# Light convolution and gated MLP on one core: first w_in columns loaded plainly, first-tile transposes ahead, tap products dealt out, early casts on GpSimd

## The chip, the cores and the metric

The kernel runs on one core of a Trainium2 chip. The metric is the device time of one execution in microseconds, lower is better. A core has TensorE (PE, with its weight loads shown as PEld), VectorE (DVE), ScalarE (ACT), GpSimd (POOL) and SyncE (SP); SP, ACT and POOL issue DMAs.

## The reference

```python
# _attn_ref: x [8, 4096, 192], weight [8 heads, 7 taps]
w = weight - np.max(weight, axis=-1, keepdims=True)
w = np.exp(w)
w = w / (np.sum(w, axis=-1, keepdims=True) + 1e-09)
x_pad = np.concatenate([np.zeros((B, pad, D)), x], axis=1)      # pad = 6
x_unf = x_pad[:, idx, :].reshape(B, S, K, H, group)
out = np.einsum('hk,bskhg->bshg', w, x_unf)
# _moe_ref: w_in [192, 2048], w_out [2048, 192], beta [2048]
h = x @ w_in
g = h * (1.0 / (1.0 + np.exp(-beta * h)))
return (g @ w_out).astype(np.float32)
```

A causal convolution of seven taps along the sequence, with a softmax over the taps of each head, is followed by two matrix products over 32768 tokens with a gated activation between them.

## The kernel before

The tokens are cut into two halves (streams s = 0 and 1) of 16384, and these into tiles of 512. Each tile is worked in steps: step 0 has 128 tokens of each stream, step 1 another 128, step 2 has 256 (these three make tile 0), then come steps of 256 up to token 2048 and steps of 512 after it. The 192 channels are split as 64 x 3 (`NK = 3`), so that 64 partitions hold one stream.

A step consists of mm1 (x @ w_in into PSUM tiles `ph`), the activation on ACT (`g`), and mm2 (g @ w_out into PSUM tiles `po`), which runs one step behind mm1 and is dealt out between its groups. There are two `ph` and two `po` buffers. When a pair of 128-token blocks has had all its mm2 products, DVE copies `po` into `o_sb` and SP stores it.

**Tile 0 is made on PE.** x0 holds its four blocks of 128 tokens of both streams. `transpose_0` turns a block with three PE transposes, `take_0` copies it into `xr[b]`, `halo_0` copies its last six columns ahead of the next block, and `conv_0` multiplies with seven tap diagonals (`diag[k]`, made by DVE from `etap`, the exponentials of the taps), accumulating in PSUM. `evac_0` scales the result by the inverse sum of the taps into `xcp`. Steps 0 to 2 use `mm1_pair`: PE's upper and lower 64 rows work on two different column groups of w_in at a time, u and u + 8, so only half s of w_in_s need hold column half s.

**Later tiles are made on DVE.** `load_x(j)` loads tile j as fp32 (`xf`, two buffers), `cast_x(j)` casts and reorders it into `xb` (two buffers), four DMA transposes (`transpose_x`, on SP) put it into `xt`, and `conv_ops` makes the convolution in seven passes: the first is a product (L291), the others multiply and add (`scalar_tensor_tensor`, L293, with inputs xt and acc). The last writes `xc`, which mm1 reads.

**Order.** Nearly every instruction is pinned in program order, so the order is written by hand. For the steps after 2, DVE's convolutions are in the list `work`. `vector_work` takes items from it by a budget of nanoseconds per PE group and an estimated cost of each item; o_sb copies are put into DVE's queue where PE's program reaches the end of a pair. Tile 1's cast and transposes are written out in step 1, those of tile 2 and later are the items of `fetch`.

**Head.** POOL's queue loads w_in in four casting DMAs (fp32 to bf16), then w_out as fp32 (`w_out_f`), then tile 1; later it issues four copies of w_in_s from one half of the partitions to the other (`copy_w_in`), which only mm1 of step 3 and later needs. DVE scales w_out_f by 1/beta into `w_out_s`, slice by slice (`scale_w_out`); all 16 slices are read by the first half of mm2 of step 0. beta comes to its place by a PE transpose. `warm` issues products of zeros while PE has nothing to do.

Of the kernel before, what the change touches and what calls it, by code (L numbers as in the profile page):

```python
# [19 lines left out]
def kernel(  # L20
# [24 lines left out]
    def pin(ins):  # L45

        return tc.keep_in_program_order(ins)
# [33 lines left out]
    def cast_x(j, s, b0=0, b1=NB, eng=None):  # L81
        if j not in xbf_of:
            xbf_of[j] = xbf_pool.tile([128, NB, NK, NS, Q], BF16, name="xb")
        pin((eng or nc.vector).tensor_copy(  # L84
            xbf_of[j][:, b0:b1, :, s, :].rearrange("p b k q -> p k b q"),
            xf_of[j][:, b0:b1, s, :].rearrange("p b (q k) -> p k b q", k=NK)))
# [29 lines left out]
    taps = consts.tile([H, K], FP32, name="taps")  # L116
    pin(nc.sync.dma_start(out=taps, in_=weight))
    x0 = consts.tile([128, NB, NS, D], FP32, name="x0")
    pin(nc.scalar.dma_start(out=x0[:, 0, 1, :], in_=xs[1, 0:128, :]))
    pin(nc.sync.dma_start(out=x0[:, 0, 0, :], in_=xs[0, 0:128, :]))  # L120
    beta16 = consts.tile([NF, 128], FP32, name="beta16")
    pin(nc.sync.dma_start(out=beta16, in_=moe_beta.rearrange("(c p) -> c p", p=128)))

# [4 lines left out]
    scrap = consts.tile([128, 1], FP32, name="scrap")  # L128
    pin(nc.scalar.activation(scrap, one, AF.Exp))

    HF = F // 2
    load_w_in(0, 0, 512)

    def load_x0(b, eng=nc.gpsimd):
        pin(eng.dma_start(out=x0[:, b, :, :],
                          in_=xs[:, 128 * b:128 * b + 128, :].rearrange("s p d -> p s d")))

    for b in range(1, NB):
        load_x0(b, nc.sync)


    sel = consts.tile([H, NS, H, Q // H], FP32, name="sel")
    pin(nc.gpsimd.memset(sel, 0.0))
    pin(nc.gpsimd.affine_select(out=sel, in_=sel, compare_op=ALU.not_equal, fill=1.0, base=0,
                                pattern=[[0, NS], [-1, H], [0, Q // H]], channel_multiplier=1))
    ident = consts.tile([128, 128], FP32, name="ident")
    pin(nc.gpsimd.memset(ident, 0.0))
    pin(nc.gpsimd.affine_select(out=ident, in_=ident, compare_op=ALU.not_equal, fill=1.0,
                                base=0, pattern=[[-1, 128]], channel_multiplier=1))
    for f in range(0, HF, 512):  # L150
        for s in range(NS):
            if f or s:
                load_w_in(s, HF * s + f, HF * s + f + 512)
    for c in range(0, NF, 4):
        pin(nc.gpsimd.dma_start(out=w_out_f[:, c:c + 4, :], in_=w_out_v[:, c:c + 4, :]))
    for b in (0, 2):
        for s in range(NS):
            load_x(1, s, b, b + 2, nc.gpsimd)
    for f in range(0, HF, 512):
        for s in range(NS):  # L160
            copy_w_in(s, HF * s + f, HF * s + f + 512)
    for s in range(NS):
        cast_x(1, s, 2, 4, nc.gpsimd)


    xr = [consts.tile([128, NK, PAD + 128], FP32R, name=f"xr{b}") for b in range(NB)]
# [4 lines left out]
    def po_tile():  # L171
        return psum_o.tile([128, 2, TILE], FP32, name="po")
# [29 lines left out]
    def transpose_0(bank, b):  # L202
        t = bank[:, 0:NK * 128].rearrange("p (k t) -> p k t", k=NK)
        v = x0[:, b, :, :].rearrange("p s d -> p (s d)").rearrange("p (m k) -> p k m", k=NK)
        for kk in range(NK):
            pin(nc.tensor.transpose(t[:, kk, :], v[:, kk, :], ident))  # L206
        return t

    def take_0(t, b, act=False):

        if act:
            pin(nc.scalar.activation(xr[b][:, :, PAD:], t, AF.Copy))
        else:
            pin(nc.vector.tensor_copy(xr[b][:, :, PAD:], t))  # L214

    def halo_0(t, b):
        dst = xr[b + 1][:, :, 0:PAD] if b + 1 < NB else xt_of[0][:, :, TILE + LEAD - PAD:]
        pin(nc.vector.tensor_copy(dst, t[:, :, 128 - PAD:]))

    def conv_0(cv, b):  # L220

        for k in range(K):
            for s in range(NS):
                pin(nc.tensor.matmul(  # L224
                    cv[s][:, 0:NK * 128], diag[half_of(s), k, :, :].rearrange("p s q -> p (s q)"),
                    xr[b][half_of(s), :, k:k + 128], start=(k == 0), stop=(k == K - 1)))
# [10 lines left out]
    def banks(po):  # L237
        return [po[:, 0, :], po[:, 1, :]]

    new_xt(0)  # L240
    po01 = po_tile()
    t0_ = transpose_0(po01[:, 0, :], 0)
    take_0(t0_, 0, act=True)
    po_b = po_tile()
    beta_ps = po_b[:, 1, 0:NF]
    pin(nc.tensor.transpose(beta_ps, beta16, ident[0:NF, 0:NF]))
    beta = consts.tile([128, NF], FP32, name="beta")
    pin(nc.vector.tensor_copy(beta, beta_ps))
    for k in range(2, K):
        make_diag(k)  # L250
    rsum = consts.tile([128, 1], FP32, name="rsum")
    pin(nc.vector.reciprocal(rsum, tsum))
    warm(3, 128)
    pin(nc.scalar.activation(scrap, one, AF.Silu))
    b0 = [cv0[:, 0, :], po_b[:, 0, :]]
    conv_0(b0, 0)
    evac_0(b0, 0, 0, nc.scalar)
    evac_0(b0, 0, 1, nc.vector)
    warm(5, 128)
# [4 lines left out]
    halo_0(t0_, 0)  # L264

    def scale_w_out(c):
        pin(nc.vector.tensor_scalar_mul(w_out_s[:, c, :], w_out_f[:, c, :], rbeta[:, c:c + 1]))  # L267
# [122 lines left out]
    def fetched(j):  # L390
        for b in range(NB):
            transpose_x(j, b)
        if (j + 2) * TILE < TS:
            for s in range(NS):
                load_x(j + 2, s)

    def fetch(i, j):
        return [(i, 850, lambda s=s: cast_x(j, s)) for s in range(NS)] + [(i, 0, lambda: fetched(j))]

    work = []  # L400
    for i in range(NP, n_steps):
# [18 lines left out]
    for i in range(n_steps):  # L420
        plan = mm2_plan(i - 1) if i else [[] for _ in range(NF)]
        g_of[i] = g_pool.tile([128, NF, NS, TILE], BF16, name="g")
        if i == 0:
            for u in range(NF // 2):
                mm1_pair(0, u)
                if u == 0:
                    t = transpose_0(po01[:, 1, :], 1)
                    take_0(t, 1)
                    halo_0(t, 1)
                elif u == 1:  # L430
                    cv = banks(po_tile())
                    conv_0(cv, 1)
                    for s in range(NS):
                        evac_0(cv, 1, s, nc.vector)
                elif u == 2:
                    po23 = po_tile()
                    t = transpose_0(po23[:, 0, :], 2)
                    take_0(t, 2)
                    halo_0(t, 2)
                elif u == 4:  # L440
                    cv = banks(po_tile())
                    conv_0(cv, 2)
                    for s in range(NS):
                        evac_0(cv, 2, s, nc.vector)
                elif u == 6:
                    t = transpose_0(po23[:, 1, :], 3)
                    take_0(t, 3)
                    halo_0(t, 3)
                if u >= 4:
                    for c in range(2 * (u - 4), 2 * (u - 3)):  # L450
                        scale_w_out(c)
            continue
        if i < NP:
            for u in range(NF // 2):
                mm1_pair(i, u)
                if i == 1 and u == 0:
                    for c in range(8, 12):
                        scale_w_out(c)
                    cv = banks(po_tile())
                    conv_0(cv, 3)  # L460
                    for c in range(12, NF):
                        scale_w_out(c)
                    for s in range(NS):
                        evac_0(cv, 3, s, nc.vector)
                for t in plan[2 * u] + plan[2 * u + 1]:
                    mm2(i - 1, *t)
                if i == 1 and u == 4:
                    for s in range(NS):
                        cast_x(1, s, 0, 2)
                    for b in range(2):  # L470
                        transpose_x(1, b)
                if i == 2:
                    vector_work(i, 1300, flush=u == NF // 2 - 1)
            if i == 1:
                for s in range(NS):
                    load_x(2, s)
                for b in range(2, NB):
                    transpose_x(1, b)
# [40 lines left out]
```

## Time and profile before

| | |
|---|---|
| time, median of three | 697.3 us (696.92 to 697.62) |
| the profiled execution's own time | 697.36 us |
| its span, first to last instruction | 695.6 us |
| PE busy | 686.9 us (99%) |
| DVE busy | 541.8 us (78%) |
| ACT busy | 587.2 us (84%) |
| POOL busy | 13.7 us (2%) |
| first mm1 product | at 9.0 us, its second half at 9.7 us |
| first product of step 3 | at 36.0 us |

The page gives each engine's busy time over the whole span. A busy PE is not a PE at its peak, since products are pipelined and their ends are modelled. A share over the whole span hides that the first 60 us have other limits than the rest, so the first 60 us are read by themselves: in the chain of waits (what released what, followed back from the end), in the busy time of stretches, and in the timeline of single instructions.

### The profile page before, as it was taken

How to read it: one execution, taken by the hardware profiler on the slowest of the kernel's cores; microseconds unless marked ns; L12 is line 12 of the kernel's file. 1: busy time of each engine (PE TensorE's matmuls, PEld its weight loads, DVE VectorE, ACT ScalarE, POOL GpSimd, SP SyncE). 2: the span in 40 equal slices, each digit the busy share in tenths (PEclk: the TensorE clock that was granted, in tenths of full speed). 3: DMA queues.
4: the chain of work that ended last, by engine and by line, in shares of the span. 5: the costliest groups of instructions: out<-in, count | busy, mean ns of one | idle time of the engine just before them, and what ended most of it. 6: DMA issues, size and time to landing. Idle time of an engine off the chain costs nothing.

```text
span 695.6 us, 25420 instructions
## 1 busy us (share of the span) xinstructions
PE 686.9 (99%) x11559; PEld 538.6 (77%) x11559; DVE 541.8 (78%) x901; ACT 587.2 (84%) x600; POOL 13.7 (2%) x26
## 2 busy tenths in 40 slices
PE   8999999999999999999999999999999999999998
PEld 6699996777777777777777777777777777777777
DVE  4799999999988788778798778797788797785002
ACT  5899999888888888888888888888888888888881
POOL 7000000000000000000000000000000000000000
PEclk9999999999999999999999999999999999999999
DMA  9654433443423334233334233334323342211112
GB/s 228 142 132 115 116 102 100 106 125 104 131 70 104 99 104 115 75 89 98 98 105 115 72 90 100 98 104 116 78 79 104 98 105 70 60 36 47 36 37 69
DMA packets 121196, 67.33 MB, mean 97 GB/s; under 512 B 55024, under 2 KB 120384, under 8 KB 121088
## 3 DMA queue, kind: packets, MB, share of 16 engines
q1 hardware_dynamic: 119152, 61.67, 32.8%
q0 software_dynamic: 1792, 3.93, 2.4%
q8 instruction: 90, 1.47, 0.9%
q14 instruction: 18, 0.15, 0.1%
q10 hardware_dynamic: 144, 0.10, 0.1%
HBM read 28.32 MB, written 25.17 MB: 77 GB/s over the span
## 4 chain that ended last, share of the span: by engine, by line
PE 92%; DVE 5%; DMA 1%; issue 1%; SPq 0%; POOL 0%; DVEq 0%; POOLq 0%
PE po L360 45%; PE ph L323 45%; DVE acc L293 3%; PE po L383 2%; DMA w_in_s<-in_moe_w_in_dram 1%; DVE w_out_s L267 1%; DVE xb L84 1%; PE po L224 0%; DVE acc L291 0%; DMA xt<-xb 0%; SPq L95 0%; DVE o_sb L368 0%; PE ph L310 0%; DVE xcp L235 0%; PE po L206 0%
## 5 line engine op out<-in xcount | busy, mean ns | idle before, releaser
L326 ACT ACTIVATE g<-ph,beta 128x1024 bf16<-128x1024 f32 (+1 forms) x544 | 560.8, 1039 | 85.0 <-PE ph L323 81.2
L360 PEld LDWEIGHTS <-g 64*128 64x128 bf16 x7936 | 361.1, 94 | 94.6 <-issue 1.3
L360 PE MATMUL po<-w_out_s,g 64*128 64x192 bf16 x7936 | 427.1, 243 | 0.7 <-DVE o_sb L368 0.5
L323 PE MATMUL ph<-xc,w_in_s 64*128 64x512 bf16 (+1 forms) x3264 | 419.0, 357 | 0.7 <-DVE xc L293 0.7
L293 DVE SCALAR_TENSOR_TENSOR acc<-xt,tapn,acc 128x512 f32<-128x512 bf16 (+1 forms) x450 | 315.4, 764 | 0.9
L323 PEld LDWEIGHTS <-w_in_s 64*128 64x128 bf16 x3264 | 167.7, 94 | 47.5 <-PE po L360 0.9
L368 DVE COPY o_sb<-po 128x384 f32<-128x384 f32 x124 | 69.1, 557 | 129.0 <-PE po L360 127.1
L293 DVE SCALAR_TENSOR_TENSOR xc<-xt,tapn,acc 128x512 bf16<-128x512 bf16 (+1 forms) x90 | 64.2, 765 | 0.2
L84 DVE CAST xb<-xf 128x768 bf16<-128x768 f32 (+1 forms) x62 | 49.0, 831 | 0.0
L291 DVE TENSOR_SCALAR acc<-xt,tapn 128x512 f32<-128x512 bf16 (+1 forms) x90 | 40.5, 501 | 3.0 <-DMA xt<-xb 1.9
L314 ACT ACTIVATE g<-ph,beta 128x256 bf16<-128x256 f32 (+1 forms) x48 | 22.0, 562 | 5.6 <-PE ph L310 5.2
L310 PE MATMUL ph<-xcp,w_in_s 64*128 64x256 bf16 (+1 forms) x144 | 14.5, 306 | 2.1 <-ACT g L314 1.5
L310 PEld LDWEIGHTS <-w_in_s 64*128 64x128 bf16 x144 | 6.9, 94 | 5.9 <-issue 3.4
L383 PE MATMUL po<-w_out_s,g 128*128 128x192 bf16 x128 | 10.7, 246 | 0.0
L383 PEld LDWEIGHTS <-g 128*128 128x128 bf16 x128 | 10.5, 98 | 0.2 <-issue 0.2
L386 DVE COPY o_sb<-po 128x192 f32<-128x192 f32 x8 | 2.9, 358 | 7.6 <-PE po L383 7.6
L235 DVE TENSOR_SCALAR xcp<-po,rsum 128x384 bf16<-128x384 f32 x7 | 4.0, 611 | 4.5 <-PE po L224 4.5
L224 PE MATMUL po<-xr,diag 64*128 64x384 f32 x49 | 7.1, 379 | 0.3 <-DVE xr L214 0.2
L224 PEld LDWEIGHTS po<-xr,diag 64*128 64x128 f32 x49 | 5.7, 204 | 1.1 <-DVE xr L214 1.1
L282 DVE COPY xt<-xt 128x18 bf16<-128x18 bf16 x28 | 4.7, 166 | 0.0
L267 DVE TENSOR_SCALAR w_out_s<-w_out_f,rbeta 128x192 bf16<-128x192 f32 x16 | 4.5, 353 | 0.0
L178 PE MATMUL ph<-zeros 128*128 128x256 bf16 (+1 forms) x16 | 3.1, 363 | 1.1 <-DVE xr L167 1.1
(44 smaller groups left out, 36.9 us busy)
## 6 DMA issues: line engine op xcount, KB each, us to landing
out_dram<-o_sb SPq DMA_DIRECT2D x124, 192.0 KB, 2.7
xf<-in_x_dram SPq DMA_DIRECT2D x60, 384.0 KB, 4.3
xt<-xb SPq DMA_TRANSPOSE x124, 2.4
w_out_f<-in_moe_w_out_dram POOLq DMA_DIRECT2D x4, 384.0 KB, 8.4
w_in_s<-in_moe_w_in_dram POOLq DMA_DIRECT2D x4, 192.0 KB, 6.6
xf<-in_x_dram POOLq DMA_DIRECT2D x4, 192.0 KB, 7.7
w_in_s<-w_in_s POOLq DMA_DIRECT2D x4, 192.0 KB, 7.0
out_dram<-o_sb SPq DMA_DIRECT2D x8, 96.0 KB, 1.6
```

Source lines behind the costliest of these rows:

```text
L84: pin((eng or nc.vector).tensor_copy(xbf_of[j][:, b0:b1, :, s, :].rearrange("p b k q -> p k b q"), xf_of[j][:, b0:b1, s, :].rearrange("p b ...
L224: pin(nc.tensor.matmul(cv[s][:, 0:NK * 128], diag[half_of(s), k, :, :].rearrange("p s q -> p (s q)"), xr[b][half_of(s), :, k:k + 128], sta ...
L267: pin(nc.vector.tensor_scalar_mul(w_out_s[:, c, :], w_out_f[:, c, :], rbeta[:, c:c + 1]))
L291: pin(nc.vector.tensor_scalar_mul(a, src, w))
L293: pin(nc.vector.scalar_tensor_tensor(out=xc_of[i][:, k0:k1, 0:n] if k == K - 1 else a, in0=src, scalar=w, in1=a, op0=ALU.mult, op1=ALU.add))
L310: pin(nc.tensor.matmul(ph[:, h, 0:NS * n], w_in_s[half_of(h), kk, ts(fcs[h], 128)], xc_of[i][half_of(h), :, kk, :], start=(kk == 0), stop= ...
L314: pin(nc.scalar.activation(g_of[i][:, fcs[h], :, 0:n], ph[:, h, 0:NS * n].rearrange("p (s t) -> p s t", s=NS), AF.Silu, scale=beta[:, fcs[ ...
L323: pin(nc.tensor.matmul(ph[:, s, 0:n], w_in_s[half_of(s), kk, ts(fc, 128)], xc_of[i][half_of(s), kk, 0:n], start=(kk == 0), stop=(kk == NK ...
L326: pin(nc.scalar.activation(g_of[i][:, fc, :, 0:n], ph[:, :, 0:n], AF.Silu, scale=beta[:, fc:fc + 1]))
L360: pin(nc.tensor.matmul(po[:, q, 0:D], g_of[i][r, fc, s, ts(b, 128)], w_out_s[r, fc, :], start=(phase == 0 and fc == 0), stop=(phase == 1 a ...
L368: pin(nc.vector.tensor_copy(o_sb, po[:, :, 0:D]))
L383: pin(nc.tensor.matmul(po[:, 0, 0:D], g_of[i][:, fc, s, ts(b, 128)], w_out_s[:, fc, :], start=(fc == 0), stop=(fc == NF - 1)))
```

## The change

- The first 256 columns of each half of w_in are loaded as fp32 by SP's queue into `w_in_f` and cast into w_in_s by DVE. POOL's casting loads shrink to 384 columns each, and POOL makes `ident` and `sel` ahead of them.
- x0's block 0 comes by one DMA of ACT's queue for both streams, blocks 1 to 3 by two DMAs of SP's queue behind w_in_f; beta16 comes last there.
- beta's transpose goes behind conv_0 of block 0, into the idle `ph` tile. The transposes of blocks 1, 2 and 3 run ahead of the first pair, behind pair 0 and behind pair 1 of step 0. Two `po` tiles, pa and pb, serve all of tile 0's transposes and convolutions.
- conv_0 of blocks 1 and 2 is cut by taps into pieces behind the pairs of step 0 (1, 3, 3 and 2, 3, 2 taps), that of block 3 into 4 and 3 behind pairs 3 and 4 of step 1. The scalings of w_out are placed anew.
- The casts of tile 1 are all on POOL: the first two ahead of the w_in copies, the other two behind them. Tile 1's transposes and tile 2's load move to the end of step 0.
- The casts of tiles 2, 3 and 4 go from DVE to POOL, and the planner counts them as 0 ns in place of 850 each.

```diff
-    pin(nc.scalar.dma_start(out=x0[:, 0, 1, :], in_=xs[1, 0:128, :]))
-    pin(nc.sync.dma_start(out=x0[:, 0, 0, :], in_=xs[0, 0:128, :]))
+    pin(nc.scalar.dma_start(out=x0[:, 0, :, :], in_=xs[:, 0:128, :].rearrange("s p d -> p s d")))
+    HF = F // 2
+    FP = 256
+    w_in_f = consts.tile([128, NK, FP], FP32, name="w_in_f")
+    for s in range(NS):
+        pin(nc.sync.dma_start(out=w_in_f[half_of(s), :, :], in_=w_in_v[:, :, HF * s:HF * s + FP]))
+    for s in range(NS):
+        pin(nc.sync.dma_start(out=x0[:, 1:, s, :],
+                              in_=xs[s, 128:TILE, :].rearrange("(b p) d -> p b d", p=128)))
...
-    for f in range(0, HF, 512):
+    for f0, f1 in ((FP, FP + 384), (FP + 384, HF)):
         for s in range(NS):
-            if f or s:
-                load_w_in(s, HF * s + f, HF * s + f + 512)
+            load_w_in(s, HF * s + f0, HF * s + f1)
...
-    def conv_0(cv, b):
-
-        for k in range(K):
+    def conv_0(cv, b, k0=0, k1=K):
+
+        for k in range(k0, k1):
...
+    pa = po_tile()
+    t = transpose_0(pa[:, 0, :], 0)
+    take_0(t, 0, act=True)
+    warm(4, 128)
     for k in range(2, K):
         make_diag(k)
     rsum = consts.tile([128, 1], FP32, name="rsum")
     pin(nc.vector.reciprocal(rsum, tsum))
-    warm(3, 128)
+    halo_0(t, 0)
+    for s in range(NS):
+        pin(nc.vector.tensor_copy(w_in_s[half_of(s), :, HF * s:HF * s + FP], w_in_f[half_of(s), :, :]))
+    for s in range(NS):
+        cast_x(1, s, 0, 2, nc.gpsimd)
+    for f in range(0, HF, 512):
+        for s in range(NS):
+            copy_w_in(s, HF * s + f, HF * s + f + 512)
+    for s in range(NS):
+        cast_x(1, s, 2, 4, nc.gpsimd)
...
+    beta_ps = idle[:, 1, 0:NF]
+    pin(nc.tensor.transpose(beta_ps, beta16, ident[0:NF, 0:NF]))
+    beta = consts.tile([128, NF], FP32, name="beta")
+    pin(nc.vector.tensor_copy(beta, beta_ps))
+    t = transpose_0(pa[:, 0, :], 1)
+    take_0(t, 1)
+    halo_0(t, 1)
...
     def fetch(i, j):
-        return [(i, 850, lambda s=s: cast_x(j, s)) for s in range(NS)] + [(i, 0, lambda: fetched(j))]
+        eng = nc.gpsimd if j <= 4 else nc.vector
+        return [(i, 850 if eng is nc.vector else 0, lambda s=s: cast_x(j, s, eng=eng)) for s in range(NS)] + [(i, 0, lambda: fetched(j))]
...
+            cv1, cv2, cv3 = banks(pb), banks(pa), banks(pb)
             for u in range(NF // 2):
                 mm1_pair(0, u)
                 if u == 0:
-                    t = transpose_0(po01[:, 1, :], 1)
-                    take_0(t, 1)
-                    halo_0(t, 1)
-                elif u == 1:
-                    cv = banks(po_tile())
-                    conv_0(cv, 1)
-                    for s in range(NS):
-                        evac_0(cv, 1, s, nc.vector)
-                elif u == 2:
-                    po23 = po_tile()
-                    t = transpose_0(po23[:, 0, :], 2)
+                    t = transpose_0(pb[:, 0, :], 2)
                     take_0(t, 2)
                     halo_0(t, 2)
...
+                elif u == 1:
+                    t = transpose_0(pa[:, 0, :], 3)
                     take_0(t, 3)
                     halo_0(t, 3)
+                    conv_0(cv1, 1, 0, 1)
+                elif u == 2:
+                    conv_0(cv1, 1, 1, 4)
+                elif u == 3:
+                    conv_0(cv1, 1, 4, K)
+                    for s in range(NS):
+                        evac_0(cv1, 1, s, nc.vector)
...
+            for b in range(2):
+                transpose_x(1, b)
+            for s in range(NS):
+                load_x(2, s)
+            for b in range(2, NB):
+                transpose_x(1, b)
             continue
```

The piece of steps 4 to 7 of the loop over u, and step 1's loop, follow the same manner as listed above.

More of the change, by code (lines that the diff above doesn't have):

```diff
@@ L129 @@
     pin(nc.scalar.activation(scrap, one, AF.Exp))
[L131 to L139, printed above, removed]
+    ident = consts.tile([128, 128], FP32, name="ident")
+    pin(nc.gpsimd.memset(ident, 0.0))
+    pin(nc.gpsimd.affine_select(out=ident, in_=ident, compare_op=ALU.not_equal, fill=1.0,
+                                base=0, pattern=[[-1, 128]], channel_multiplier=1))
     sel = consts.tile([H, NS, H, Q // H], FP32, name="sel")
@@ L145 @@
                                 pattern=[[0, NS], [-1, H], [0, Q // H]], channel_multiplier=1))
[L146 to L149, printed above, removed]
-    for f in range(0, HF, 512):
+    for f0, f1 in ((FP, FP + 384), (FP + 384, HF)):
         for s in range(NS):
-            if f or s:
-                load_w_in(s, HF * s + f, HF * s + f + 512)
+            load_w_in(s, HF * s + f0, HF * s + f1)
     for c in range(0, NF, 4):
@@ L158 @@
             load_x(1, s, b, b + 2, nc.gpsimd)
-    for f in range(0, HF, 512):
-        for s in range(NS):
-            copy_w_in(s, HF * s + f, HF * s + f + 512)
-    for s in range(NS):
-        cast_x(1, s, 2, 4, nc.gpsimd)
     xr = [consts.tile([128, NK, PAD + 128], FP32R, name=f"xr{b}") for b in range(NB)]
@@ L240 @@
     new_xt(0)
[L241 to L248, printed above, removed]
+    pa = po_tile()
+    t = transpose_0(pa[:, 0, :], 0)
+    take_0(t, 0, act=True)
+    warm(4, 128)
     for k in range(2, K):
@@ L252 @@
     pin(nc.vector.reciprocal(rsum, tsum))
-    warm(3, 128)
+    halo_0(t, 0)
[8 more added lines that the diff above has]
+        cast_x(1, s, 2, 4, nc.gpsimd)
     pin(nc.scalar.activation(scrap, one, AF.Silu))
-    b0 = [cv0[:, 0, :], po_b[:, 0, :]]
+    pb = po_tile()
+    b0 = [cv0[:, 0, :], pb[:, 0, :]]
     conv_0(b0, 0)
@@ L258 @@
     evac_0(b0, 0, 1, nc.vector)
-    warm(5, 128)
+    beta_ps = idle[:, 1, 0:NF]
[5 more added lines that the diff above has]
+    halo_0(t, 1)
     rbeta = consts.tile([128, NF], FP32, name="rbeta")
@@ L263 @@
     pin(nc.vector.tensor_scalar_mul(tapn, etap, rsum))
-    halo_0(t0_, 0)
     def scale_w_out(c):
@@ L426 @@
                 if u == 0:
-                    t = transpose_0(po01[:, 1, :], 1)
-                    take_0(t, 1)
-                    halo_0(t, 1)
-                elif u == 1:
-                    cv = banks(po_tile())
-                    conv_0(cv, 1)
-                    for s in range(NS):
-                        evac_0(cv, 1, s, nc.vector)
-                elif u == 2:
-                    po23 = po_tile()
-                    t = transpose_0(po23[:, 0, :], 2)
+                    t = transpose_0(pb[:, 0, :], 2)
                     take_0(t, 2)
                     halo_0(t, 2)
[L440 to L446, printed above, removed]
+                elif u == 1:
+                    t = transpose_0(pa[:, 0, :], 3)
                     take_0(t, 3)
                     halo_0(t, 3)
-                if u >= 4:
-                    for c in range(2 * (u - 4), 2 * (u - 3)):
-                        scale_w_out(c)
+                    conv_0(cv1, 1, 0, 1)
[5 more added lines that the diff above has]
+                        evac_0(cv1, 1, s, nc.vector)
+                elif u == 4:
+                    conv_0(cv2, 2, 0, 2)
+                elif u == 5:
+                    conv_0(cv2, 2, 2, 5)
+                    for c in range(4):
+                        scale_w_out(c)
+                elif u == 6:
+                    conv_0(cv2, 2, 5, K)
+                    for s in range(NS):
+                        evac_0(cv2, 2, s, nc.vector)
+                elif u == 7:
+                    for c in range(4, 8):
+                        scale_w_out(c)
+            for b in range(2):
+                transpose_x(1, b)
+            for s in range(NS):
+                load_x(2, s)
+            for b in range(2, NB):
+                transpose_x(1, b)
             continue
@@ L455 @@
                 mm1_pair(i, u)
-                if i == 1 and u == 0:
-                    for c in range(8, 12):
+                if i == 1 and u < 2:
+                    for c in range(8 + 4 * u, 12 + 4 * u):
                         scale_w_out(c)
[L459 to L462, printed above, removed]
+                elif i == 1 and u == 3:
+                    conv_0(cv3, 3, 0, 4)
+                elif i == 1 and u == 4:
+                    conv_0(cv3, 3, 4, K)
                     for s in range(NS):
-                        evac_0(cv, 3, s, nc.vector)
+                        evac_0(cv3, 3, s, nc.vector)
                 for t in plan[2 * u] + plan[2 * u + 1]:
                     mm2(i - 1, *t)
[L467 to L471, printed above, removed]
                 if i == 2:
@@ L474 @@
             if i == 1:
[L475 to L478, printed above, removed]
                 for s in range(NS):
```

## The prediction

> **What bounds the kernel now.** I read the chain of waits first, from 23 to 60 us, then the busy time by stretch, then single instructions in the timeline.
>
> ```profile
> PE 92%; DVE 5%; DMA 1%; issue 1%; SPq 0%; POOL 0%; DVEq 0%; POOLq 0%
> ```
>
> The 5% is not spread out. The chain lies on VectorE almost without a break from 16 us to 58 us, and on PE from there to the end:
>
> ```profile
> 23.24 0.81 DVE xb L84 x2
> 24.07 2.23 SPq L95
> 26.35 2.36 DMA xt<-xb
> 28.79 0.76 DVE acc L291
> ...
> 35.78 1.60 DVE xb L84 x2
> ...
> 44.62 1.60 DVE xb L84 x2
> ```
>
> Columns are start, length, what. Tile 1 is cast on DVE at 23.2, transposed by DMA, and from 28.8 the tap convolutions run; the casts of tiles 2 and 3 stand between them, on the chain. By stretch (length, then PE, PEld, DVE, ACT, POOL busy):
>
> ```profile
> 36.00:47.60 11.60, 11.06 (x232) 10.87 (x233) 11.39 (x16) 11.29 (x18) 0.00 (x0) 1.00 0.43 108
> 58.50:75.00 16.50, 16.50 (x354) 16.48 (x355) 16.15 (x20) 16.25 (x25) 0.00 (x0) 1.00 0.44 122
> ```
>
> DVE is full at first, PE afterwards: after 58.7 us PE has no gap worth counting. What this change is worth is therefore how much earlier or later PE enters its closed stretch. It is held up last here (the bracket gives idle time before and its releaser):
>
> ```profile
> 36.01 0.50 PE L323 MATMUL ph<-xc,w_in_s 64*128 64x256 bf16 x6 [0.71 <-DVE xc L293]
> 47.59 0.51 PE L360 MATMUL po<-w_out_s,g 64*128 64x192 bf16 x8 [0.53 <-DVE o_sb L368]
> ```
>
> At 47.59 the second product of step 3 needs the PSUM tile that o_sb number 3 empties; that copy stands in DVE's queue behind the convolutions. A last gap of 0.3 us follows at 58.4.
>
> **What the Trainium skill says.** "SBUF — State Buffer", § Who interferes with whom: VectorE and GpSimd share one pair of SBUF ports under an exclusive lock. A DVE instruction in a two-port mode, or one with two SBUF inputs against a GpSimd instruction that reads SBUF, waits for the whole of the other. The trace agrees for the first kind. A w_out_s scaling takes 0.309 us (median); this one met a POOL cast:
>
> ```profile
> 19.72 0.75 POOL L84 CAST xb<-xf 128x384 bf16<-128x384 f32 x1 [0.63 <-DMA xf<-in_x_dram]
> 19.83 0.76 DVE L267 TENSOR_SCALAR w_out_s<-w_out_f,rbeta 128x192 bf16<-128x192 f32 x1
> ```
>
> It ended 0.11 us after the cast. POOL got in although DVE's scalings stand back to back. The second kind, the taps (L293 reads xt and acc, both in SBUF), never meets a POOL instruction in this trace. "GPSIMD Engine Reference", § 7 prices a read with a step over 8 bytes at 2.9 cycles per element of a 1.2 GHz clock: 1.86 us for the 768 elements of a cast here (step 12 bytes), an estimate. The trace has 0.687 and 0.748 us for 384 elements, so I take 1.3 us for 768, with 1.2 to 1.5 as ends. "VectorE: DVE Perf Modes", § The perf-mode tier table, gives fp32 SBUF copies up to 2x; the cast of 768 strided elements measured 0.845 us on DVE. I take 0.45 to 0.85 us for one of the two new w_in casts.
>
> **The change, part by part.** The sum is against the profiled execution: span 695.6, time 697.36 us, 0.06 above the median of 697.3.
>
> *Head (0 to 9.7 us).* Before, PE waited 0.59 us for beta, conv_0 of block 0 began at 5.54, and the first pair could not finish its second half before the w_in load landed at 9.64. After: beta's transpose goes behind conv_0, which then starts at about 4.9 (xr from ACT ends 4.83) and ends at about 7.5 (2.6 us as before). The diagonals follow at 0.24 us each from 4.09, ahead of PE. On DVE the halo and two w_in casts (0.9 to 1.7 us) come before the evacuation, so xcp is ready at 7.9 to 8.4. First pair: 8.7, a gain of about 1.0. Unknown is when x0's blocks 1 to 3 and beta land: SP's queue now has two w_in loads ahead of them; the last such load landed 6.0 us after its issue at 3.1, now two issue at about 2.0 and 2.5, so 7.5 to 9.2. Ends of the gain: 0 and 1.3. One warm run of five and one of three give way to one of four; that saves nothing of weight, as PE works then anyway. POOL makes ident first, but tap_ps still needs sel, at about 2.6 as now. The same w_in bytes are read ahead of w_out_f, by two queues in place of one, so w_out_f lands where it did, about 12.7 to 16.4. At nothing I cost x0's block 0 as one ACT DMA (two halves landed by 3.2 before; the transposes wait for the tap product at 3.4 anyway) and the shared PSUM tiles pa and pb (0.3 us of waits for DVE's takes is in step 0 below; without the cover of ACT's activations it would be up to 1 us).
>
> *Step 0.* Eight pairs at 0.33, two transposes at 0.45, two convs at 1.37 dealt out by taps: 6.3 us of PE, 6.6 with bank waits, against 18.12 - 9.68 = 8.4. ACT no longer idles 1.25 us behind a whole conv. Step 1 starts at 15.3.
>
> *Step 1.* Now the w_out chain binds: evacuation of block 2 ends at 15.9, twelve scalings at 0.23 make 18.7. But tile 1's first casts are now POOL's, and land-bound at 17.0 to 18.4: two locks of 0.7 put the last slice at 20.1, and mm2 of step 0 waits for it (it ended at 22.5 before). Left on PE: five pairs 1.65, conv 1.37, second half of mm2 1.4: 24.5 against 26.06, a gain of 1.55.
>
> *Convolution of tile 1.* Before, it waited for the last evacuation, two casts and two DMA transposes until 28.79. Now POOL casts by 18.4, transposes issue then and take the 4.7 us of before (24.07 to 28.79), up to 6.7 while the DMA engines are still full: 23.1 to 25.1. o_sb number 1 ends at 25.0. So DVE starts the taps at 25.2, **3.6 us earlier**. POOL's w_in copies slide to 18.4-20.9, needed only at step 3: free. o_sb 1's store now stands behind tile 2's loads and two transposes on SP, at about 27 as before; four o_sb buffers cover it. Step 2 is ACT's 16 activations, 9.35 us, so step 3 can't start before 33.75 (35.3 before).
>
> *DVE up to o_sb number 3.* The compiled order puts it behind conv 3 (7.0), first product and two taps (2.85), o_sb 2 (0.46), four taps (4.2), halo (0.15), product and four taps (4.95), itself (0.5): 20.1 us, so 45.3 against PE's 47.59. The fetch now costs the planner nothing, so four more taps stand ahead of this copy than before; that is why 3.6 became 2.3.
>
> *The six casts of tiles 2, 3, 4 on POOL.* They leave 3.2 us of casts (tiles 2, 3) off DVE ahead of that copy, already counted in the 20.1. When do they run? Loads of tile 2 issue at about 22.1 behind the first transposes and land 3.5 and 5.0 us later, as before: 25.7 and 27.6. Tile 3's follow o_sb 1's store: 30 and 32. Tile 4's come behind tile 2's four transposes (5.9 us on SP): 39.5 and 41. All six fall into the taps ahead of o_sb 3. If a tap waits for a POOL cast, each costs DVE 1.3, six 7.8, less about 0.6 where one falls on a first product or a PSUM copy, which have one SBUF input or none: 7.2. Then conv 3 ends at about 37, step 3 starts there and not at 33.75, and o_sb 3 ends at 52.5: PE is **4.9 later** than at 47.59, 4.6 with the gap at 58.4 gone. After it DVE has no POOL beside it and keeps up (conv 6 and o_sb 5 end at about 63.0, needed at 63.4), so the loss stays constant. Sum: 697.36 + 4.6 = **702.0**.
>
> **Rivals.** (A) *Taps are locked out by POOL's casts*: the case above. For it: the collision shown and the page's plain rule. Against: no tap has met one here. 699.8 to 704.0, from locks of 1.1 to 1.5 us and one us either way in the start of the taps.
> (B) *Taps run beside POOL.* If the rule doesn't hold for this operation, or DVE keeps the lock through its row of taps, the casts are hidden: o_sb 3 at 45.3, -2.3, and -0.3 for the later gap: **694.7** (693.5 to 695.8). It decides between A and B at 2.6/6 = 0.43 us of lock per cast. For it: POOL is empty from 20 us on and the taps start 3.6 us earlier.
> (C) *A part is locked*, as where casts land beside evacuations or come after o_sb 3: two of six, 2.6 us, 697.4, no change.
> (D) *The head gives nothing back*, because x0 lands after 9.2 behind the w_in loads: moves A or B up by up to 1 us, less where the w_out chain binds.
>
> **How the numbers follow.** A 0.66, B 0.24, C 0.10; D lies in their widths. 0.2% is 1.4 us, about what a measurement of this kernel can tell from no change. Faster takes B without its upper end, 0.23; same 0.09; slower the rest, 0.68. The range must reach B to leave out no more than 2 in 10: 694.2 to 704.0; A's own is 699.8 to 704.0. Predicted: 702.0.
>
> **What would show it.** Right: taps (L294) of 2.0 to 2.4 us beside POOL casts, in place of 1.02; PE waiting for xc at about 37 and for o_sb at about 52; the first tap near 25. Wrong: taps of 1.02 us beside the casts, or the wait for o_sb at 45. The head is wrong if the first pair starts after 9.6, the w_out chain if mm2 of step 0 runs before 19.

## The result and the profile after

The changed kernel is slower. Its median is 706.26 us (703.83 to 706.52, four runs) against 697.46 us for the kernel before (696.92 to 698.49, four runs): ratio 1.0117, 95% interval 1.0091 to 1.0142. The profiled execution took 706.52 us at a span of 704.7, so it is 9.1 us of span above the one of before; it is the slowest of the four. The forecast had the sign and the lock of VectorE by GpSimd, missed how late the first loads land, and had half of the amount.

From the page of the kernel after: the shares of the chain, then three groups (busy us, mean ns | idle before, releaser).

```profile
PE 94%; DVE 3%; DMA 1%; issue 1%; SPq 0%
L361 PE MATMUL po<-w_out_s,g 64*128 64x192 bf16 x7936 | 429.2, 243 | 3.1 <-DVE o_sb L369 2.9
L84 POOL CAST xb<-xf 128x768 bf16<-128x768 f32 (+1 forms) x10 | 11.9, 1217 | 19.4 <-DMA xf<-in_x_dram 19.3
L256 PE MATMUL ph<-ident,beta 16*128 16x16 f32 x1 | 0.3, 282 | 5.1 <-DMA beta<-in_moe_beta_dram 5.1
```

DVE's share of the chain fell from 5% to 3%, which alone would look like progress. Two waits have grown: one tiny transpose of beta idles PE for 5.1 us (0.59 before), and one o_sb copy holds the second product of step 3 up for 2.9 us (0.53 before). The chain of waits of the kernel after, start, length, what:

```profile
3.73 8.79 DMA beta<-in_moe_beta_dram
...
20.55 0.61 DVE xcp L225
21.16 1.98 DVE w_out_s L268 x4
...
32.22 0.76 DVE acc L292
...
37.22 1.88 DVE acc L294
39.16 1.75 issue
40.91 0.75 DVE acc L292
```

Its first long piece is an 8 KB load, and it enters the taps at 32.22, where the chain of before entered them at 28.79. The same places in PE's timeline of the kernel after (the bracket gives idle time before and its releaser):

```profile
12.56 0.28 PE L256 MATMUL ph<-ident,beta 16*128 16x16 f32 x1 [5.07 <-DMA beta<-in_moe_beta_dram]
...
13.62 0.82 PE L311 MATMUL ph<-xcp,w_in_s 64*128 64x256 bf16 x6
...
41.13 0.50 PE L324 MATMUL ph<-xc,w_in_s 64*128 64x256 bf16 x6 [0.54 <-DVE xc L294]
...
55.39 0.51 PE L361 MATMUL po<-w_out_s,g 64*128 64x192 bf16 x8 [2.88 <-DVE o_sb L369]
```

The first pair starts at 13.62 (8.98 and 9.68 before), step 3 at 41.13 (36.01 before), and the wait for o_sb number 3 ends at 55.39 (47.59 before). Six products take 0.82 us at 13.62 and 0.50 at 41.13.

**The taps beside POOL.** A tap is one multiply-and-add pass of `conv_ops`. VectorE's timeline and then GpSimd's, of the kernel after:

```profile
33.01 6.08 DVE L294 SCALAR_TENSOR_TENSOR acc<-xt,tapn,acc 128x768 f32<-128x768 bf16 x5
39.12 1.86 DVE L294 SCALAR_TENSOR_TENSOR xc<-xt,tapn,acc 128x768 bf16<-128x768 bf16 x1
...
44.14 4.59 DVE L294 SCALAR_TENSOR_TENSOR acc<-xt,tapn,acc 128x768 f32<-128x768 bf16 x3
```

```profile
28.90 2.47 POOL L84 CAST xb<-xf 128x768 bf16<-128x768 f32 x2 [6.34 <-DMA xf<-in_x_dram]
36.53 3.65 POOL L84 CAST xb<-xf 128x768 bf16<-128x768 f32 x2 [5.16 <-DMA xf<-in_x_dram]
43.73 3.13 POOL L84 CAST xb<-xf 128x768 bf16<-128x768 f32 x2 [3.56 <-DMA xf<-in_x_dram]
```

Tile 2's casts ran alone, 1.22 us each, ahead of the taps. Each of the other four met a tap: four taps took 1.87, 1.86, 1.64 and 1.87 us in place of 1.02, together 3.2 us more (taken singly; the lines above have them in groups). The casts grew as well (3.65 and 3.13 for two). A lock means here what these lines show: a VectorE instruction that meets a GpSimd cast takes longer, and mostly the cast does too.

Last, the busy time by stretch (length, then PE, PEld, DVE, ACT, POOL, granted clock, DMA share, GB/s):

```profile
32.20:55.30 23.10, 18.93 (x335) 15.63 (x331) 22.52 (x23) 20.55 (x33) 6.78 (x4) 1.00 0.59 155
56.50:59.90 3.40, 3.40 (x42) 3.20 (x38) 3.33 (x5) 1.98 (x4) 0.00 (x0) 0.50 0.33 101
60.00:75.00 15.00, 15.00 (x324) 14.98 (x321) 12.48 (x15) 14.85 (x23) 0.00 (x0) 1.00 0.21 53
```

DVE is nearly full from 32.2 to 55.3 (22.52 of 23.10 us), as it was before; PE is full from 60 on. Between them lies what before did not have: 3.4 us with PE's granted clock at half (0.50), soon behind the o_sb wait.

**The 9.1 us in one sum.** Taps start at 32.22 against 28.79: +3.4. From there to the end of o_sb number 3 it takes 23.1 us (55.34 - 32.22) against 18.7 (47.53 - 28.79): +4.4, of which the locks are 3.2 and the rest, 1.2 to 1.3, is four more taps ahead of the copy (about 4.2) less the four casts of tiles 2 and 3 that left DVE (about 3.0). So PE leaves its wait 7.8 later. The gap of 0.3 us at 58.4 is gone, and half a clock for 3.4 us costs the remaining 1.6.

### The profile page after: what moved, and what is told of

The parts are those of the page before. It is cut to its first block, busy times and chain, and to the rows that moved or that the text cites. A ratio compares the mean times of both kernels' runs of the same rounds, so it can differ in the third digit from the quotient of the medians.

```text
span 704.7 us, 25423 instructions
## 1 busy us (share of the span) xinstructions
PE 690.3 (98%) x11555; PEld 540.6 (77%) x11555; DVE 542.5 (77%) x895; ACT 587.6 (83%) x600; POOL 24.1 (3%) x34
## 4 chain that ended last, share of the span: by engine, by line
PE 94%; DVE 3%; DMA 1%; issue 1%; SPq 0%
PE po L361 46%; PE ph L324 45%; DVE acc L294 2%; PE po L384 2%; DMA beta<-in_moe_beta_dram 1%; PE ph L311 1%; PE po L214 0%; PE po L197 0%; DVE acc L292 0%; DVE w_out_s L268 0%; DVE xcp L225 0%; SPq L124 0%; SPq L126 0%; DVE o_sb L369 0%; SPq L117 0%
## 5 line engine op out<-in xcount | busy, mean ns | idle before, releaser
L84 DVE CAST xb<-xf 128x768 bf16<-128x768 f32 x54 | 43.3, 844 | 0.0
L84 POOL CAST xb<-xf 128x768 bf16<-128x768 f32 (+1 forms) x10 | 11.9, 1217 | 19.4 <-DMA xf<-in_x_dram 19.3
L214 PE MATMUL po<-xr,diag 64*128 64x384 f32 x49 | 9.1, 428 | 0.0
```

Of the source, the lines that this page charges most:

```text
L84: pin((eng or nc.vector).tensor_copy(xbf_of[j][:, b0:b1, :, s, :].rearrange("p b k q -> p k b q"), xf_of[j][:, b0:b1, s, :].rearrange("p b ...
L214: pin(nc.tensor.matmul(cv[s][:, 0:NK * 128], diag[half_of(s), k, :, :].rearrange("p s q -> p (s q)"), xr[b][half_of(s), :, k:k + 128], sta ...
```

## The experiments

Twelve further kernels were run. Each ratio is against runs of the kernel before on the same chip (medians there 697.46 to 698.24); the places in us come from one profiled execution each.

| kernel | median us | ratio, 95% interval | taps start | step 3 starts | o_sb 3 ends |
|---|---|---|---|---|---|
| before (profiled once) | 697.46 | 1 | 28.79 | 36.01 | 47.53 |
| after | 706.26 | 1.0117, 1.0091 to 1.0142 | 32.22 | 41.13 | 55.34 |
| e1_casts_dve | 700.93 | 1.0042, 1.0030 to 1.0054 | 32.01 | 40.30 | 50.77 |
| b1_casts_pool | 705.32 | 1.0103, 1.0082 to 1.0124 | 29.53 | 38.42 | 54.55 |
| e2_pairs_first | 704.45 | 1.0103, 1.0077 to 1.0128 | 32.92 | 41.83 | 55.97 |
| e3_warm | 703.70 | 1.0098, 1.0068 to 1.0127 | 29.40 | 39.30 | 53.50 |
| e4_pairs_dve | 699.54 | 1.0025, 1.0012 to 1.0038 | 29.90 | 38.18 | 48.64 |
| p1_pool_reads | 703.17 | 1.0069, 1.0049 to 1.0089 | 29.68 | 39.40 | 53.25 |
| p2_pool_writes | 699.69 | 1.0027, 1.0018 to 1.0037 | 29.10 | 36.32 | 49.21 |
| b2_tile1_early | 698.37 | 0.9996, 0.9987 to 1.0005 | 28.69 | 36.97 | 47.42 |
| g1_cost850 | 701.13 | 1.0054, 1.0041 to 1.0067 | 31.35 | 40.27 | 50.46 |
| f1_loads_before | 699.84 | 1.0027, 1.0017 to 1.0038 | 30.68 | 38.98 | 49.43 |
| f2_loads_dve2 | 696.95 | 0.9990, 0.9981 to 0.9999 | 27.42 | 35.72 | 46.17 |
| f3_before_early | 697.64 | 0.9999, 0.9989 to 1.0009 | 29.51 | 37.79 | 48.24 |

### The casts alone, taken back and put in

e1_casts_dve is the kernel after with the casts of tiles 2 to 4 on DVE again. b1_casts_pool is the kernel before with only those casts on POOL, at 0 ns, the very line of the change.

```diff
-        eng = nc.gpsimd if j <= 4 else nc.vector
-        return [(i, 850 if eng is nc.vector else 0, lambda s=s: cast_x(j, s, eng=eng)) ...
+        return [(i, 850, lambda s=s: cast_x(j, s)) ...
```

> The changed kernel with one part undone: the casts of tiles 2, 3 and 4 are back on DVE at 850 ns each for the planner. Theory (late head, then port lock, then order): the head stays late, so the taps of tile 1 still start near 32.2 us; the four lock waits (3.2 us together) and the four taps put ahead of o_sb 3 (1.3 us) go, DVE's own casts stand on the chain as before, o_sb 3 ends near 50.9, PE's wait for it falls from 2.9 us to under 0.5 and its clock doesn't drop afterwards (1.6 us): about 701.0 us, 5.5 less than the changed kernel. Rival 1 (the casts on POOL pay, everything lost is the head): DVE takes back 3.2 us of casts, 707 to 709 us. Rival 2 (the long taps have another cause than POOL): taps of 1.87 us remain, within 1 us of the changed kernel.

> The kernel before with one part of the change alone: the casts of tiles 2, 3 and 4 on POOL, 0 ns for the planner. Theory: the taps start near 28.8 as before, all six casts meet taps, each lengthens one by 0.85 us (5.1), four more taps stand ahead of o_sb 3 (1.3): it ends near 53.9, PE waits over 3.4 us there and its rate drops for a while (up to 1.6): 703.5 to 705.5 us. Rival 1 (only the head makes the changed kernel slow; a hidden cast relieves DVE): 696 to 697. Rival 2 (order alone, no lock): +1.3, 698.5.

Both came as the lock theory had them: taking the casts back leaves 0.4% of the 1.2%, and the casts alone make 1.0% in a kernel whose head is untouched. VectorE's timeline of e1, then of b1:

```profile
32.80 5.24 DVE L294 SCALAR_TENSOR_TENSOR acc<-xt,tapn,acc 128x768 f32<-128x768 bf16 x5
38.07 1.02 DVE L294 SCALAR_TENSOR_TENSOR xc<-xt,tapn,acc 128x768 bf16<-128x768 bf16 x1
39.01 1.59 DVE L84 CAST xb<-xf 128x768 bf16<-128x768 f32 x2
```

```profile
30.32 6.90 DVE L293 SCALAR_TENSOR_TENSOR acc<-xt,tapn,acc 128x768 f32<-128x768 bf16 x5
...
38.19 1.70 DVE L291 TENSOR_SCALAR acc<-xt,tapn 128x768 f32<-128x768 bf16 x1
39.92 2.64 DVE L293 SCALAR_TENSOR_TENSOR acc<-xt,tapn,acc 128x768 f32<-128x768 bf16 x2
...
46.09 1.87 DVE L293 SCALAR_TENSOR_TENSOR xc<-xt,tapn,acc 128x768 bf16<-128x768 bf16 x1
47.88 1.19 DVE L282 COPY xt<-xt 128x18 bf16<-128x18 bf16 x1
```

In b1 all six casts met an operation: four taps (+0.85, +0.82, +0.56, +0.85), a first product (1.70 against 0.75) and a halo copy (1.19 against 0.16), in sum 5.1 us or 0.84 a cast. Compare e1: two casts on DVE take 1.59 us, 0.80 a cast. So a cast moved to POOL still costs DVE about what it had cost there.

g1_cost850 keeps the casts on POOL and lets the planner count them at 850, as it did while they were DVE's. It tells the order from the locks.

```diff
-        return [(i, 850 if eng is nc.vector else 0, lambda s=s: cast_x(j, s, eng=eng)) ...
+        return [(i, 850, lambda s=s: cast_x(j, s, eng=eng)) ...
```

> The changed kernel with one number changed: the planner counts POOL's casts as 850 ns each as before, not 0; they stay on POOL. That sets o_sb 3 back behind the first product of its convolution, four taps earlier. Theory: the head and the four lock waits stay (taps from 32.2 us, step 3 near 41.1), o_sb 3 ends near 51.3 in place of 55.3, before PE needs it at 52.0; PE's wait of 2.9 us goes and its rate doesn't drop there: 701 to 702.5 us. Rival (the wait is the locks' alone, the order is worth its 1.3 us or less): 704.5 to 705.5.

VectorE's timeline of g1:

```profile
32.13 6.08 DVE L294 SCALAR_TENSOR_TENSOR acc<-xt,tapn,acc 128x768 f32<-128x768 bf16 x5
38.25 1.87 DVE L294 SCALAR_TENSOR_TENSOR xc<-xt,tapn,acc 128x768 bf16<-128x768 bf16 x1
...
41.16 6.92 DVE L294 SCALAR_TENSOR_TENSOR acc<-xt,tapn,acc 128x768 f32<-128x768 bf16 x5
```

The locks are all still there (four taps, 3.4 us more than 5.24 and 1.02 allow), yet the kernel is as fast as e1, and PE waits for no o_sb. o_sb number 3 ends 19.1 us behind the start of the taps (50.46 - 31.35), against 18.8 in e1 and 23.1 in after. So the locks were paid for by the casts taken off; the loss of after over e1 came from dealing out four more taps ahead of o_sb number 3, as if DVE had gained the time. The 0 in the budget was the error, as much as the engine.

### What a POOL instruction costs a DVE one

Two kernels are the kernel before with spare work on POOL behind the loads of tile 2, which nothing reads: six casts like those of the change (p1), or six memsets (p2, behind two one-column casts that set the same start).

```diff
+                for n in range(6):
+                    sp = consts.tile([128, NB, NK, Q], BF16, name=f"spare{n}")
+                    pin(nc.gpsimd.tensor_copy(sp.rearrange("p b k q -> p k b q"), xf_of[2][:, :, n % NS, :]...))
```

```diff
+                for n in range(6):
+                    sp = consts.tile([128, 1024], FP32, name=f"spare{n + 1}")
+                    pin(nc.gpsimd.memset(sp, 0.0))
```

> The disputed cost alone: the kernel before, and besides six spare POOL casts of tile 2's xf (768 elements, as the real ones) into tiles that nothing reads, from the landing of tile 2 on. Theory (a tap with two SBUF inputs is locked out by a POOL instruction that reads SBUF): six DVE instructions of the taps become longer by 0.85 us, 5 us in all, and the time rises by 4 to 6.5 us. Rival (no lock): taps stay at 1.02 us, the time at 697.4.

> The counterpart: the kernel before, and besides two one-column POOL casts (for the same start) and six POOL memsets of 1024 fp32 columns, which write SBUF and read none. Theory: memsets share no read port, taps stay at 1.02 us but for one or two at the start, 697.4 to 698. Rival (any POOL instruction holds DVE up): taps lengthen as with the casts, 4 us or more.

The timelines of POOL and DVE, first of p1, then of p2:

```profile
32.83 10.37 POOL L483 CAST spare<-xf 128x768 bf16<-128x768 f32 x6 [12.40 <-DMA xf<-in_x_dram]
30.46 6.92 DVE L293 SCALAR_TENSOR_TENSOR acc<-xt,tapn,acc 128x768 f32<-128x768 bf16 x5
37.42 1.83 DVE L293 SCALAR_TENSOR_TENSOR xc<-xt,tapn,acc 128x768 bf16<-128x768 bf16 x1
39.17 3.25 DVE L84 CAST xb<-xf 128x768 bf16<-128x768 f32 x2
42.34 1.41 DVE L291 TENSOR_SCALAR acc<-xt,tapn 128x768 f32<-128x768 bf16 x1
```

```profile
34.05 6.29 POOL L486 MEMSET spare<- 128x1024 f32 x6
29.89 5.24 DVE L293 SCALAR_TENSOR_TENSOR acc<-xt,tapn,acc 128x768 f32<-128x768 bf16 x5
36.09 2.54 DVE L84 CAST xb<-xf 128x768 bf16<-128x768 f32 x2
```

In p1 three taps (1.83 to 1.87), two casts (1.81 and 1.51 against 0.85) and a first product (1.41 against 0.75) grew by 4.8 us together; the median grew by 4.9 (703.17, of two runs, against 698.24). In p2 the taps kept 1.02 beside the memsets, but casts (1.35 and 1.27) and the first product (1.15) grew, 1.3 us together, and the median by 1.4. The lock theory had p2 nearly free (697.4 to 698) and missed by about that much: it knew only the taps. In these two runs the casts and the first product, with one SBUF input, wait beside POOL's casts and beside its memsets; the taps, with two, only beside its casts, which read SBUF.

### The head

e2_pairs_first puts beta's load second on SP and the transposes of blocks 1 to 3 behind pairs 2 and 3; e4_pairs_dve is e2 with the casts of tiles 2 to 4 on DVE. e3_warm is after with twenty products of zeros in PE's idle stretch.

```diff
+    beta16 = consts.tile([NF, 128], FP32, name="beta16")
+    pin(nc.sync.dma_start(out=beta16, ...))        # e2: ahead of the w_in_f loads
...
-    t = transpose_0(pa[:, 0, :], 1)                # e2: behind pair 2
```

```diff
     evac_0(b0, 0, 1, nc.vector)
+    warm(20, 256)
```

> The changed kernel with only the wait at the head taken away: beta is loaded second on SP's queue, and the transposes of blocks 1 to 3 stand behind pairs 2 and 3 of step 0 in place of ahead of pair 0 and behind pairs 0 and 1 (the pieces of the convolutions follow later). Theory: the first pair starts near 9.0 us in place of 13.7, PE waits about 1.7 us for x0 behind pair 2, step 1 starts near 18.4 in place of 22.8, the taps near 28.1 (then bound by the second transpose's landing). But now all six POOL casts meet taps, 5.1 us of lock in place of 3.2, so o_sb 3 ends near 53.1 and the time is about 704, only 2 less. Rival (the head is nearly the whole loss): 4.5 us less, 701.5 to 702. Rival (PE's wait at the head is covered by something later anyway): no change, 706.

> The changed kernel with 20 products of zeros put between conv_0 of block 0 and beta's transpose, where PE stands idle for 5 us. Theory: the wait for beta stays (first pair near 13.7 us), but PE is not at half rate from 13 to 19 us: a pair takes 0.33 in place of 0.76 us, step 1 starts some 2 us earlier (near 21), the taps near 30.3; one more POOL cast then meets a tap (0.85 us), so the time gains 0.8 to 1.5 us: about 705.3. Rival (the slow pairs are ACT's or the products' waits and not PE's rate): pairs stay at 0.76, 706.4.

> Both at once on the changed kernel: pairs first with beta early (no wait at the head) and the casts of tiles 2 to 4 on DVE. Theory: the taps start near 28.1 and without lock o_sb 3 ends near 46.7, 0.8 earlier than in the kernel before, and the gap at 58 goes: 696.3 us, level with the kernel before or a little under it. What is left of the change is then worth about 1 us. Rival (there is a third loss, as in the dealt-out convolutions or the shared PSUM tiles): 698.5 or more.

e2 did what it should to the first pair (8.91), but against after its time gained nothing clear of the noise (the intervals overlap). It fits its forecast only by chance: in the profiled execution, the slowest of its four, the taps start at 32.92 and not near 28.1. The first reason is in PE's timeline of e2:

```profile
12.91 1.52 PE L197 MATMUL po<-ident,x 128*128 128x128 f32 x6 [1.42 <-DMA x<-in_x_dram]
```

x0's later blocks are just as late as beta, so with beta out of the way PE waits for them; and from 25.3 to 28.7 its clock is granted at half. e3 removes what the waiting does to PE: from 7.5 us on PE ran at its full rate, step 1 began at 19.04 in place of 22.84 and the taps at 29.40. In that run beta landed 1.2 us earlier, so about 2.6 of the 3.8 are the rate, an estimate. Its gain at the end is not certain; the intervals of e3 and of after overlap. e4 missed (696.3 was expected): x0 landed at 12.3 again, and step 1 held at 19.6.

f1_loads_before therefore undoes all the loads: no w_in_f, w_in, x0 and beta as in the kernel before, the rest of the change kept, casts of tiles 2 to 4 on DVE.

```diff
-    for s in range(NS):
-        pin(nc.sync.dma_start(out=w_in_f[half_of(s), :, :], ...))
...
+    load_w_in(0, 0, 512)
+    for b in range(1, NB):
+        load_x0(b, nc.sync)
```

> The changed kernel without the plain load of w_in (loads of w_in, x0 and beta in the order and sizes of the kernel before, no casts of w_in on DVE) and with the casts of tiles 2 to 4 on DVE. What is left: transposes ahead, convolutions dealt out by taps, tile 1 brought forward. Theory (the late x0 and beta are the w_in loads' doing): x0's block 1 lands near 7.4 and beta near 4.9 as before, the first pair starts near 9.7, step 1 near 16.5 and not 22.8, step 3 near 35.2: 695.5 to 696.5 us. Rival (the dealt-out order loses by itself, or POOL's casts lock the w_out scalings too long): 698 or more.

The head came back: block 1 is transposed at 7.6 and the first pair starts at 8.48, its second half at 9.83. The time did not, which is a miss: against e1, from which it differs by the loads and what belongs to them, the taps start 1.3 us earlier, but the intervals of the two ratios overlap, so it isn't certain that undoing the loads gains time. Three things remained. PE ran at half its rate until 16.0, where before had the full rate from 9.7. POOL's second casts of tile 1 meet the scalings of w_out. And PE's granted clock is at half from 22.8 to 26.2, where before has none such up to 75 us. The timelines of POOL, DVE and PE in f1:

```profile
21.16 1.37 POOL L84 CAST xb<-xf 128x384 bf16<-128x384 f32 x2
20.37 4.34 DVE L270 TENSOR_SCALAR w_out_s<-w_out_f,rbeta 128x192 bf16<-128x192 f32 x12
23.04 0.87 PE L313 MATMUL ph<-xcp,w_in_s 64*128 64x256 bf16 x6
```

f2_loads_dve2 takes the second of these away: tile 1's second casts go to DVE ahead of o_sb number 1 and their transposes to the end of step 1; its first casts stay on POOL, now behind the w_in copies.

```diff
-    for s in range(NS):
-        cast_x(1, s, 2, 4, nc.gpsimd)
+    for s in range(NS):
+        cast_x(1, s, 0, 2, nc.gpsimd)
...
+                    for s in range(NS):
+                        cast_x(1, s, 2, 4)
```

> As the last, and tile 1's second casts on DVE where it waits for o_sb 1, with the w_in copies ahead of POOL's two remaining casts. Theory: w_out's scalings meet two POOL casts in place of four (0.5 to 1.3 us less on the way to step 2) and the transposes land earlier; step 3 near 34.5 to 35: 695 to 696 us, the fastest of all. Rival: no gain over the last one, as the scalings wait for their loads.

From DVE's timeline of f2, then the end of step 2 in its chain of waits:

```profile
19.32 2.82 DVE L268 TENSOR_SCALAR w_out_s<-w_out_f,rbeta 128x192 bf16<-128x192 f32 x12
...
25.49 0.90 DVE L84 CAST xb<-xf 128x384 bf16<-128x384 f32 x2
...
27.42 0.75 DVE L292 TENSOR_SCALAR acc<-xt,tapn 128x768 f32<-128x768 bf16 x1
```

```profile
27.46 9.37 ACT g L315 x16
36.87 0.50 PE ph L324 x6
```

Twelve scalings in 2.82 us, taps 1.4 us earlier than before, no wait for o_sb number 3 at 46.17: at 0.9990 f2 has the lowest ratio of all, but its interval barely excludes 1, and with thirteen ratios in the table one such is no proof of a gain. How much of the 2.9 us between f1 and f2 are the scalings, and how much the stretch at half clock, which f2's profile does not have there, was not separated. In f2 the chain has left DVE: step 2's activations on ACT set when step 3 goes on, as the prediction's step 2 had it. That fits a gain of no more than about 0.7 us from taps that start 1.4 earlier. The second change of f2 was not tried with the loads of after, so the loads' own share stays open.

### The early tile 1 alone

b2_tile1_early and f3_before_early are the kernel before with tile 1's casts and transposes early. In b2 all four casts are on POOL ahead of the w_in copies, and tile 2's load is early too; in f3 the first two are on POOL behind the copies and the second two on DVE.

```diff
+    for b in (0, 2):                               # b2
+        for s in range(NS):
+            cast_x(1, s, b, b + 2, nc.gpsimd)
...
-                        cast_x(1, s, 0, 2)         # f3: the second casts at this place
+                        cast_x(1, s, 2, 4)
```

> The kernel before with tile 1 alone brought forward: all four of its casts on POOL ahead of the w_in copies, its transposes and tile 2's load at the end of step 0; everything else as before. Theory: the transposes land near 23, the taps start behind o_sb 1, near 27.0 to 27.6 in place of 28.8 (two more casts may lock w_out's scalings, up to 0.7 us); PE's waits of 0.7, 0.5 and 0.3 us go: 695.8 to 696.5 us. Rival (the scalings are locked for longer and step 1 ends later): 697.4 or more.

> The kernel before with the smallest piece of the change: tile 1's first two casts on POOL (behind the w_in copies) and its first two transposes at the end of step 0; its last two casts on DVE, where DVE waits for o_sb 1. Theory: the taps no longer wait for cast and transposes, they start right behind o_sb 1, near 27.0 in place of 28.8; as the w_out scalings meet two POOL casts as before, step 1 is not longer; step 3 at 35.3: 695.8 to 696.4 us. Rival (PE's waits for ACT in step 2 take its place): 697.2.

Both missed: no difference (0.9996 and 0.9999), where 1 to 2 us were expected. In b2 the first four scalings took 2.68 us in place of 1.00 beside POOL's casts, and PE waited 1.80 us for DVE's take of block 3; in f3 the first four scalings took 2.39, that wait was 1.50 us, and PE's clock was at half from 20.0 to 23.4. So in the order of before the early casts push DVE's work for tile 0 back; f2, which has the change's finer order in step 0, starts its taps earlier than both.

## Why the prediction was right and wrong

- **Sign and lock: right.** Rival A, taps locked out by POOL's casts, is shown by e1, b1 and p1, against B (taps beside POOL) and C. Where the prediction looked for taps of 2.0 to 2.4 us beside POOL's casts they were 1.64 to 1.87, and the wait for o_sb that it put at 52 ended at 55.4.
- **The head: the step that failed.** It put x0's blocks and beta at 7.5 to 9.2 us and the first pair at 8.7, from one load of 192 KB that landed 6.0 us after its issue, though each of the new x0 loads has 288 KB; behind two w_in loads the last x0 blocks landed at 12.3 and beta at 12.5. Rival D capped this at 1 us. It did not ask what stands behind beta's transpose in PE's queue: the first pair and all of step 0. The first pair started at 13.6, step 1 at 22.8, not 15.3, and the taps at 32.2, not 25.2. The loads are only a part of that: with them undone the taps are at 30.7 (f1) against 32.0 (e1). Beside them f1 shows PE's half rate and POOL's casts at the w_out scalings; the shares stay open. The two w_in casts took 0.93 and 0.95 us, more than the 0.45 to 0.85 allowed; the wait for beta covered it. That two w_in_f loads and not POOL's smaller w_in loads delay x0 was not separated.
- **PE's rate in the head, put at nothing.** Behind the 5.07 us wait PE did not come to its full rate before 18.9, and by e3 about 2.6 us of step 1's delay are the rate. That the fewer warm runs ("saves nothing of weight") have a part in it isn't shown: of f1 and f2, whose heads are alike, one had the half rate until 16.0, the other the full rate from 9.9 to 12.2 and the half rate until 15.4.
- **The lock: right in kind, mis-sized.** Six locks of 1.3 less 0.6 made 7.2. A cast costs DVE 0.84 (b1), less than the 1.22 us that it takes alone, and POOL's cast pays too: three of the four took 1.74 to 1.96 us. Why the loss is smaller than the cast isn't shown. Only four of six met anything in the kernel after, since the late head left tile 2's casts ahead of the taps: 3.2 us in all. The discount for a first product was wrong, since it is locked as well. The estimate from "GPSIMD Engine Reference", § 7, in the Trainium skill was 1.86 us for the cast; the trace has 1.22.
- **The order: right.** 20.1 us of DVE work up to o_sb number 3 was forecast without locks; 23.1 less 3.2 makes 19.9. g1 shows that this order turns the casts into a loss: with all the locks but the order of before it is as fast as e1.
- **PE's rate behind the wait for o_sb: not foreseen.** It cost 1.6 us.
- In sum: the head 7.0 too early, locks 4.0 and order 0.2 too dear, rate 1.6 left out: 7.0 - 4.0 - 0.2 + 1.6 = 4.4 of the 4.5 between 702.0 and the profiled 706.5. Two errors partly hid each other.

## What to carry to other kernels

Here moving casts from VectorE to GpSimd was no gain while VectorE was full. In such a case measure the lock per instruction beside what the move takes off, and charge it to the order's budget, since a 0 there makes the planner put more work ahead of the copy that PE waits for. When loads are put ahead of others in a queue, add up what then lands last, and look in each in-order engine for the first instruction that needs it, however small: 8 KB of beta held all of PE. In the kernel after, two idle stretches on PE cost more than their length, so price the slow products behind one too.

## What was not expected of the hardware

- VectorE operations with one SBUF input (a cast of 768 elements, 0.85 us alone; a first product, 0.75 alone) are locked as well, beside POOL's casts and beside its memsets (p1, p2). "SBUF — State Buffer", § Who interferes with whom, in the Trainium skill says so of operations in a two-port mode; the durations alone did not tell that these are in one.
- After a PE wait of 2.88 us the granted clock went to half for 3.4 us, 1.1 us after work had resumed. "TensorE: Matmul & The Clock Gate", Part 1, in the Trainium skill gives about 3.4 us of idling as what takes the clock to half. Here the measurement differs: this wait was shorter, in b1 the clock fell at 38.1, before a wait of 2.83 us had ended, and in f3 and e2 waits of 1.50 us went ahead of such a stretch. In f1 no single wait in the 3 us before one was over 0.5 us. The four times of after spread over 2.7 us where those of before spread over 1.6; that these stretches make the spread isn't shown. From 12.6 to 18.9 us of the kernel after the granted clock reads 1.00 although six products take 0.82 us and not 0.50: durations of like products are the safer sign.
